# Windowed attention and a gated feed-forward block on one Trainium2 core: batch 2's q and k transposed by DMA, a new order of loads, batch 1 by token halves

## Chip, core and metric

The kernel runs on one core of one Trainium2 chip. The metric is the device time of one execution in microseconds (us). A profiled execution also has a span, from the first to the last recorded instruction; it is some 1.7 us shorter than the time. All executions compared below are in the fast state: none was over 1.5% above the fastest of its kernel, and the mean granted TensorE clock of a run was 0.96 to 1.0 of full speed.

## The reference

```python
# B, H, S, D = 4, 8, 768, 64;  n_sink = 4, window = 128
scores = (1 / sqrt(D)) * q @ k.T                 # per batch and head
keep   = is_sink(key) | (0 <= query - key < window)
a      = softmax(where(keep, scores, -1e9))
x      = (a @ v)           -> [3072, 512]        # tokens x (heads * D)
out    = (((x @ w1) * (x @ w2)) @ w3) @ w_out    # 512 -> 1024 -> 1024 -> 512
```

Inputs and output are fp32. A query sees four "sink" keys at the start and the 128 newest keys, so of the six key blocks of 128 only two and a strip are needed for each query block. Nothing stands between `@ w3` and `@ w_out`, so the kernel multiplies these two once into one matrix (the "fold") and uses that.

## The kernel before

All inputs are cast to bf16 while a DMA loads them. TensorE does, for each batch: transposes of q and k (so that the head dimension lies on partitions), score matmuls on 64 partitions, attention-value matmuls, transposes of x, then for each half of 384 tokens sixteen groups of four "gate" matmuls (w1 and w2) and the projection with the fold. VectorE and ScalarE share exps, masks, normalisation and the copies out of PSUM.

The order of instructions on each engine is not written by hand. Every piece of work is recorded as an `Op` with an estimated duration, its dependencies and the buffers that it takes; a list scheduler keeps a planned timeline (the "plan" below) and emits the operation that can start first:

```python
class Op:
    def __init__(self, eng, us, fn, deps=(), prio=0.0, takes=(), frees=(), ...): ...
# GpSimd issues the casting loads in exactly this order: k/q/v <batch>-<block>,
# w3j, w3 and wo: parts of w3 and w_out; w0..w3: quarters of w1 and w2
LOADS = """ident k0-0-4 q0-0-4 v0-2 w3j-0-1 tri v0-0 pick v0-1 wo-1-2 w3j-2-4 wo-0-1 w3j-1-2 wo-2-4
    w3j-4-6 wo-4-6 w3j-6-8 wo-6-8 w3-3 w3-5 w3-7 w2 w3-6 w0 w3-4 w3 k0-1-0 q0-1-0 v0-4 v0-3 ..."""
QK_BY_DMA, X_BY_DMA = (3,), (2, 3)     # batches whose q, k / whose x are transposed by DMA

# ... transposes of q and k of one batch, where TensorE does them: 2 x 4 groups of 6
a = Op(PE, cols(P, 6), tps, [...] + war, when(r / 4 + c / 50 - 0.1, 0), takes=["mm"])
tp_of[c, r] = Op(EITHER, (act_us(6 * P), dve_us(6 * P, 2)), tpc, [a], ...)     # the copy out of PSUM
# ... and where SyncE's queue does them: 12 DMA transposes of 128 x 512
nc.sync.dma_start_transpose(out=T[:, :, s, kb * P:(kb + 1) * P], in_=src[b][:, kb, :])

# ... the values of the four sink keys, spread to the rows where they are needed
def sv(b=b, x=x):
    nc.tensor.matmul(x[0].slot["mm"][:].rearrange("p (h d) -> p h d", d=D),
                     sel[:].rearrange("p r m -> p (r m)"), vN[b][:, 0, :, 0:D], start=True, stop=True)

# ... kind 0: attention for one half of the tokens, then for the other; kind 1: by heads over all tokens
kind = 0 if b == 0 else 1

# ... filler: TensorE multiplies zeros in gaps that the plan has before 45 us
if e == PE and start < 45.0 and start - free[PE] > 0.12:
    ...
        nc.tensor.matmul(view, zeros[:], zeros[:], start=True, stop=True)

# ... the last output tile leaves in two pieces of 256 columns
for n0, n1 in ([(0, 256), (256, 512)] if last else [(0, 512)]):
    ...
```

`EITHER` lets the scheduler choose VectorE or ScalarE. PSUM is shared: two double buffers `sc` for scores and the fold, one `av` for values, three `mm` for everything else.

The softmax here doesn't subtract the row's maximum and nothing guards it: scores larger than these inputs give would overflow.

## Time and profile before

| | before |
|---|---|
| time, median of the runs beside the changed kernel's | 203.46 us (203.09 to 203.55, 4 runs) |
| span of the profiled run | 201.6 us |
| mean granted TensorE clock | 0.997 |
| first gate matmul | 31.0 us |
| last matmul ends | 198.25 us |

The page's first rows give the busy time of each engine, and its chain rows say which engine ended last, followed back from the end. The prediction below shows those rows, the chain in order of time, the groups by shape, and the tail. In the group rows the second figure after the bar is the mean duration of one instruction, from start to end (219 ns for a 128-column transpose); what it costs TensorE in a stream is the smaller distance to the next start, 55.5 ns.

### The profile page before, as it was taken

What the parts mean: (1) busy time and instruction counts of PE and PEld (TensorE: products, weight loads), DVE (VectorE), ACT (ScalarE), POOL (GpSimd) and SP (SyncE); (2) the same over time, 40 slices, a digit from 0 to 9 for tenths busy, and PEclk for the clock granted to TensorE, in tenths of its full rate; (3) what the DMA queues carried; (4) which work ended last, traced back from release to release, by engine and by line L of the source; (5) the groups of instructions that cost most, each with busy time, mean ns of one, the idle gap of its engine ahead of it and who ended that gap; (6) DMA issues with size and microseconds to landing.
All of it is one profiled execution on the core that took longest, in us unless ns stands there. A gap on an engine that the chain in (4) does not pass through costs nothing.

```text
span 201.6 us, 4577 instructions
## 1 busy us (share of the span) xinstructions
PE 196.2 (97%) x1852; PEld 120.2 (60%) x1852; DVE 110.0 (55%) x252; ACT 108.3 (54%) x175; POOL 72.9 (36%) x96
## 2 busy tenths in 40 slices
PE   7999999999999999999999999999999999999993
PEld 6666555566676676666665654665565456556442
DVE  2586212377778989858876572884484214324200
ACT  3786634388578688984455354555532343343232
POOL 7976565488999899843000000000000000000000
PEclk9999999999999999999999999999999999999998
DMA  6999999999999999999999454101123630020124
GB/s 167 166 180 201 203 202 194 177 176 156 152 195 170 157 147 131 122 170 152 155 156 123 34 101 141 44 0 52 55 71 61 132 150 8 0 105 4 52 104 156
DMA packets 91349, 24.81 MB, mean 123 GB/s; under 512 B 80192, under 2 KB 87744, under 8 KB 91328
## 3 DMA queue, kind: packets, MB, share of 16 engines
q0 software_dynamic: 73584, 14.29, 96.1%
q1 hardware_dynamic: 17200, 9.84, 21.7%
q10 hardware_dynamic: 544, 0.39, 0.6%
q8 instruction: 14, 0.23, 0.5%
q14 instruction: 7, 0.06, 0.1%
HBM read 29.36 MB, written 6.29 MB: 177 GB/s over the span
## 4 chain that ended last, share of the span: by engine, by line
PE 91%; DMA 4%; POOL 1%; DVE 1%; ACT 0%; issue 0%; ACTq 0%; DVEq 0%
PE mm L679 42%; PE mm L709 20%; PE av L599 7%; PE sc L528 6%; PE mm L359 4%; DMA big<-in_moe_w_dram 3%; PE mm L432 3%; PE sc L329 2%; PE mm L635 1%; PE mm L352 1%; DMA out_dram<-o_sb 1%; PE mm L793 1%; PE mm L329 1%; PE mm L409 1%; PE mm L321 1%; POOL early L157 1%
## 5 line engine op out<-in xcount | busy, mean ns | idle before, releaser
L679 PE MATMUL mm<-xT,w_sb 128*128 128x384 bf16 x512 | 92.3, 326 | 0.0
L679 PEld LDWEIGHTS <-w_sb 128*128 128x128 bf16 x512 | 47.7, 98 | 33.3 <-issue 2.5
L694 DVE TENSOR_TENSOR ab<-a_sb,mm 128x384 bf16<-128x384 f32 x64 | 35.2, 552 | 43.8 <-PE mm L679 42.2
L541 ACT ACTIVATE ex<-sc 128x768 bf16<-128x768 f32 (+2 forms) x52 | 44.2, 895 | 7.7 <-PE sc L528 7.3
L709 PE MATMUL mm<-w3o,ab 128*128 128x512 bf16 (+1 forms) x200 | 46.4, 370 | 0.1
L140 ACT COPY a_sb<-mm 128x384 f32<-128x384 f32 x54 | 25.8, 481 | 37.6 <-PE mm L679 25.1
L547 DVE TENSOR_TENSOR am<-ex,maskt 128x768 bf16<-128x768 bf16 (+2 forms) x52 | 30.0, 595 | 1.3 <-ACT ex L541 1.2
L709 PEld LDWEIGHTS <-ab 128*128 128x128 bf16 x200 | 18.8, 98 | 18.2 <-issue 0.8
L140 ACT COPY o_sb<-mm 128x512 f32<-128x512 f32 (+1 forms) x23 | 13.1, 568 | 25.6 <-PE mm L709 23.4
L157 POOL DMA_DIRECT2D vN<-in_v_dram x24 | 21.4, 894 | 7.1 <-DMA big<-in_k_dram 2.7
L599 PE MATMUL av<-vN,am 128*128 128x65 bf16 x352 | 18.9, 193 | 0.0
L599 PEld LDWEIGHTS <-am 128*128 128x128 bf16 x352 | 16.9, 97 | 3.1 <-issue 0.5
L614 DVE TENSOR_TENSOR xs<-av,rec 128x384 bf16<-128x384 f32 x32 | 17.7, 553 | 0.6
L528 PE MATMUL sc<-qkT 64*128 64x256 bf16 (+1 forms) x248 | 14.8, 243 | 0.0
L140 ACT COPY qkT<-mm 128x384 bf16<-128x384 bf16 (+1 forms) x20 | 12.0, 642 | 4.4 <-PE mm L432 2.6
L599 PE MATMUL av<-vsb,es 128*128 128x130 bf16 x64 | 12.8, 219 | 0.0
L528 PEld LDWEIGHTS <-qkT 64*128 64x128 bf16 x248 | 8.1, 95 | 5.9 <-issue 4.5
L157 POOL DMA_DIRECT2D big<-in_k_dram x12 | 10.8, 904 | 1.2 <-PE mm L465 0.5
L157 POOL DMA_DIRECT2D big<-in_q_dram x12 | 10.8, 902 | 0.4 <-issue 0.2
L359 PE MATMUL mm<-big,w3t 128*128 128x512 bf16 x40 | 9.8, 379 | 0.0
L609 DVE RECIPROCAL rec<-av 128x6 f32<-128x6 f32 x32 | 6.2, 193 | 5.8 <-PE av L599 5.7
L140 DVE COPY a_sb<-mm 128x384 f32<-128x384 f32 x10 | 5.6, 555 | 6.7 <-PE mm L679 6.7
(65 smaller groups left out, 149.3 us busy)
## 6 DMA issues: line engine op xcount, KB each, us to landing
out_dram<-o_sb SPq DMA_DIRECT2D x23, 256.0 KB, 2.0
vN<-in_v_dram POOLq DMA_DIRECT2D x24, 128.0 KB, 7.0
w_sb<-in_moe_w_dram POOLq DMA_DIRECT2D x8, 256.0 KB, 10.1
big<-in_k_dram POOLq DMA_DIRECT2D x12, 128.0 KB, 7.1
big<-in_q_dram POOLq DMA_DIRECT2D x12, 128.0 KB, 7.2
big<-in_moe_w_dram POOLq DMA_DIRECT2D x5, 256.0 KB, 9.1
big<-in_moe_w_out_dram POOLq DMA_DIRECT2D x3, 256.0 KB, 7.9
near<-in_q_dram POOLq DMA_DIRECT2D x6, 128.0 KB, 6.7
```

The source lines that it names most:

```text
L140: (nc.scalar.copy if turn_of[0] == ACT else nc.vector.tensor_copy)(out, in_)
L157: op = Op(eng, us, lambda: (nc.gpsimd if eng == POOL else nc.sync).dma_start(out=out, in_=in_), deps)
L359: nc.tensor.matmul(x[2].slot["mm"][:], x[1].slot["w3t"][:, j, :], wo_sb[:, j, :], start=(j == 0), stop=(j == KFF - 1))
L528: nc.tensor.matmul(sc[:, e, c * P:(c + n) * P], T[hp, r, 0, kb * P:(kb + 1) * P], T[hp, r, 1, qb * P:(qb + n) * P], start=True, stop=True)
L541: nc.scalar.activation(y[1].slot["ex"][:, :, 0:w], y[0].slot[key][:, :, 0:w], ACTF.Exp, scale=scale)
L547: nc.vector.tensor_mul(y[2].slot["am"][:, :, 0:w], y[1].slot["ex"][:, :, 0:w], maskt[:, :, m0:m0 + w].to_broadcast([P, 2, w]))
L599: nc.tensor.matmul(o, lhs, rhs, start=(i == 0), stop=(i == len(todo) - 1), skip_group_check=True)
L609: nc.vector.reciprocal(x[1].slot["rec"][:], av_of(x[0].slot["av"])[:, :, :, D:VW])
L614: nc.vector.tensor_mul(xs_first[c].slot["xs"][:, :, r * P:(r + 1) * P].rearrange("p k (e d) -> p k e d", d=D), av_of(x[0].slot["av"])[:, : ...
L679: nc.tensor.matmul(pg[:, 0:TOK], w_sb[:, kk, dt * P:(dt + 1) * P], holder[0].slot["xT"][:, kk, :], start=(kk == 0), stop=(kk == NP - 1))
L694: nc.vector.tensor_mul(abh[0].slot["ab"][:, dt, :], y[1].slot["a"][:], y[2].slot["mm"][:, 0:TOK])
L709: nc.tensor.matmul(x[0].slot["mm"][:, 0:n1 - n0], abh[0].slot["ab"][:, kk, mi * P:(mi + 1) * P], w3o[:, kk, n0:n1], start=(kk == 0), stop= ...
```

## The change

The intent is to take 48 transposes of q and k and four sink matmuls from TensorE, the limit, and to give some of the freed time back to 24 transposes of x that DMA had done before. The loads are reordered so that the earliest work gets its data first, and loads of batch 3 are meant to stay behind those of batch 2 while batch 2's DMA transposes run. Batch 1 works by token halves, so its first half can go on before the second is loaded. The rest are small things: the tail in three pieces, value rows of even width, other weights in the scheduler's priorities (`LEAD`, `SPREAD`, `FOLD_J`, `FOLD_I`).

```diff
+    VP = D + 2
-    sel = home("sel", [P, H // 2, 32])
+    vst = home("vst", [P, B, D], FP32)
-    KA, LEAD, SPREAD = 3, -50, 0.8
-    QK_BY_DMA, X_BY_DMA = (3,), (2, 3)
+    KA, LEAD, SPREAD = 3, -120, 0.6
+    FOLD_J, FOLD_I = 990, 980
+    C_MAJOR = 2
+    QK_BY_DMA = (2, 3)
+    X_BY_DMA = ((3, 0), (3, 1))
 ... [eight small DMAs put the sink rows of v into vst]
+    LOADS = """w3j-1-2 tri k0-0-4 q0-0-4 wo-0-1 wo-2-4 ident v0-2 w3j-2-4 w3j-6-8 w3j-0-1 wo-1-2 pick
+        v0-1 wo-4-6 w3j-4-6 v0-0 w3-7 wo-6-8 w3-6 w3-5 w3-4 q0-1-0 k0-1-0 w0 w3-3 v0-5 w2 v0-3 w1
+        k1-1 k1-0 w3 k1-3 q1-1 v0-4 k1-2 q1-0 q2-0 q1-2 ... v3-0 v3-5"""
 ...
-        return t[:, 0:QC * 2 * VW].rearrange("p (k e d) -> p k e d", e=2, d=VW)
+        return t[:, 0:QC * 2 * VP].rearrange("p (k e d) -> p k e d", e=2, d=VP)
 ...
-        kind = 0 if b == 0 else 1
+        kind = 0 if b < C_MAJOR else 1
 ...
+            if b + 1 in QK_BY_DMA:                      # the hold
+                seen = []
+                for o in in_big:
+                    if o.batch == b:
+                        seen.append(next(t for t in tp_of.values() if o in t.deps))
+                    elif o.batch == b + 1:
+                        o.deps += seen[:-3]
 ...
-        def sv(b=b, x=x):
-            nc.tensor.matmul(x[0].slot["mm"][:] ..., sel[:] ..., vN[b][:, 0, :, 0:D], start=True, stop=True)
+        def sv(b=b, V=V):                               # VectorE, straight from vst
+            nc.vector.tensor_mul(V ..., vst[:, b:b + 1, :] ..., pick ...)
-        groups = [(2, 3), (3, 6)] if b < 1 else [(2, 6)]
+        groups = [(2, 3), (3, 6)] if kind == 0 else [(2, 6)]
 ...
-                for n0, n1 in ([(0, 256), (256, 512)] if last else [(0, 512)]):
+                for n0, n1 in ([(0, 256), (256, 384), (384, 512)] if last else [(0, 512)]):
 ... [the last piece is copied by ScalarE and issued on ScalarE's queue]
 ... [the scheduler keeps lists of ready operations instead of scanning all]
```

More of the change, by code (lines that the diff above doesn't have):

```diff
@@ L86 @@
         kN[b] = big[:, o + NQ:o + 2 * NQ].rearrange("p (k n) -> p k n", n=DM)
-    vN = homes("vN", B, [P, NB, H, VW + 1])
+    vN = homes("vN", B, [P, NB, H, VP])
     vsb = homes("vsb", 2, [P, NP, 2, VW])
@@ L212, with sink_v @@
     Op(DVE, 0.1, lambda: nc.vector.memset(zeros[:], 0.0))
+    op_v0 = Op(DVE, 0.3, lambda: nc.vector.memset(vst[:], 0.0), prio=-1)
+    op_vst = []
+    for h in range(H):
+        def sink_v(h=h):
+            p0 = 32 * (h // 2) + 4 * (h % 2)
+            nc.sync.dma_start(out=vst[p0:p0 + 4, :, :], in_=v[:, h, 0:4, :].rearrange("b s d -> s b d"))
+        op_vst.append(Op(SP, 0.45, sink_v, [op_v0], prio=-1))
+        op_vst[-1].turn = 0.05
     op_i1 = Op(DVE, 0.17, lambda: nc.vector.memset(ident[:], 1.0))
@@ L225 @@
                                          first_home[i][:, 0:TOK].rearrange("p (h m) -> p h m", h=2), st[i])
-    LOADS = """ident k0-0-4 q0-0-4 v0-2 w3j-0-1 tri v0-0 pick v0-1 wo-1-2 w3j-2-4 wo-0-1 w3j-1-2 wo-2-4
-        w3j-4-6 wo-4-6 w3j-6-8 wo-6-8 w3-3 w3-5 w3-7 w2 w3-6 w0 w3-4 w3 k0-1-0 q0-1-0 v0-4 v0-3
-        v1-3 w1 v0-5 q1-0 k1-3 k1-1 q1-1 k1-2 k1-0 v1-0 k1-4 q1-2 q1-4 k1-5 v1-2 q1-3 q1-5 v1-5
-        k2-2 k2-1 q2-1 v1-1 v1-4 k2-0 q2-0 k2-3 k2-4 q2-4 q2-2 k2-5 q2-5 v2-0 q2-3 k3-0 v2-4 v2-1
-        v2-2 v2-5 q3-0 v2-3 k3-1 q3-1 k3-2 q3-2 k3-3 q3-5 k3-5 q3-4 k3-4 v3-0 q3-3 v3-1 v3-4 v3-3
-        v3-2 v3-5"""
+    LOADS = """w3j-1-2 tri k0-0-4 q0-0-4 wo-0-1 wo-2-4 ident v0-2 w3j-2-4 w3j-6-8 w3j-0-1 wo-1-2 pick
+        v0-1 wo-4-6 w3j-4-6 v0-0 w3-7 wo-6-8 w3-6 w3-5 w3-4 q0-1-0 k0-1-0 w0 w3-3 v0-5 w2 v0-3 w1
+        k1-1 k1-0 w3 k1-3 q1-1 v0-4 k1-2 q1-0 q2-0 q1-2 k1-4 v1-0 q1-4 v1-5 k2-0 v1-2 v1-4 k2-3
+        v1-1 q1-5 k2-2 q2-2 v1-3 q2-4 q2-1 q1-3 k2-1 k1-5 v2-5 v2-2 k2-5 v2-0 k2-4 v3-1 q2-5 q2-3
+        q3-0 k3-3 v2-4 k3-2 v2-1 v2-3 k3-0 k3-4 k3-5 q3-2 k3-1 v3-2 q3-5 q3-1 v3-4 q3-3 q3-4 v3-3
+        v3-0 v3-5"""
     def masks(part):
@@ L250, in pick_cols @@
     def pick_cols():
-        nc.vector.memset(sel[:], 0.0)
-        for e in range(2):
-            nc.vector.tensor_copy(sel[0:4, :, 4 * e:4 * e + 4],
-                                  ident[0:4, None, 0:4].to_broadcast([4, NP, 4]))
         for i in range(2):
@@ L283 @@
                 kN if key[0] == "k" else qN, k if key[0] == "k" else q, n[0], n[1])
+            late.batch = n[0]
             if n[0] > 1:
@@ L295 @@
     op_mask = Op(DVE, 0.6, lambda: masks(1), [op_mask], prio=3)
-    op_sel = Op(DVE, 1.3, pick_cols, [op_pick, op_ident], prio=3)
+    op_cols = Op(DVE, 0.35, pick_cols, [op_pick], prio=3)
     op_bd = [Op(DVE, 0.11, lambda b=b: nc.vector.memset(ksbd[b][:], 0.0), prio=3 + 20 * b) for b in range(B)]
@@ L305, in av_of @@
     def av_of(t):
-        return t[:, 0:QC * 2 * VW].rearrange("p (k e d) -> p k e d", e=2, d=VW)
+        return t[:, 0:QC * 2 * VP].rearrange("p (k e d) -> p k e d", e=2, d=VP)
     fold_done = []
     hold = [None]
+    ACC = {3: ["sc", "mm"], 4: ["sc", "av", "mm"], 5: ["sc", "sc", "av"], 6: ["sc", "sc", "av", "mm"]}[KA]
+    acc_keys, n = [], 0
+    for i, name in enumerate(ACC):
+        wide = 2 if name == "sc" else 1
+        acc_keys.append((n, wide, (name, i) if ACC.count(name) > 1 else name))
+        n += wide
     def acc_of(n):
-        return hold[0].slot["mm"][:] if n == KA - 1 else hold[0].slot["sc"][:, n, :]
+        n0, wide, key = [a for a in acc_keys if a[0] <= n][-1]
+        t = hold[0].slot[key]
+        return t[:, n - n0, :] if wide == 2 else t[:]
     last = None
@@ L330, in fm @@
                                  start=(j == 0), stop=(j == KFF - 1), skip_group_check=True)
-        a = Op(PE, cols(P, KA), t3, [got["w3j", j], op_ident], 50 + j, takes=["mm"])
+        a = Op(PE, cols(P, KA), t3, [got["w3j", j], op_ident], FOLD_J + j, takes=["mm"])
         x.append(a)
-        cpy = Op(EITHER, (act_us(KA * P), dve_us(KA * P, 2)), t3c, [a], 50 + j, takes=["w3t"], frees=[(a, "mm")])
+        cpy = Op(EITHER, (act_us(KA * P), dve_us(KA * P, 2)), t3c, [a], FOLD_J + j, takes=["w3t"], frees=[(a, "mm")])
         x.append(cpy)
         last = Op(PE, cols(DM, KA), fm, [cpy, got["wo", j]] + ([last] if last else []),
-                  50.5 + j, takes=["sc", "mm"] if j == 0 else [], frees=[(cpy, "w3t")])
+                  FOLD_J + 0.5 + j, takes=ACC if j == 0 else [], frees=[(cpy, "w3t")])
         if j == 0:
@@ L340 @@
     first_fm = hold[0]
-    for i0, n_i, key in ((0, 2, "sc"), (2, 1, "mm")):
+    for i0, n_i, key in acc_keys:
         def fe(i0=i0, n_i=n_i, key=key):
@@ L363, in fmc @@
             copy(w3o[:, i, :], x[2].slot["mm"][:])
-        pr = 100 + 4 * i
+        pr = FOLD_I + 4 * i
         a = Op(PE, cols(P, KFF), t3, [got["w3", i], op_ident], pr, takes=["mm"])
@@ L440 @@
                            [got[n, b, QC * c + j] for n in "kq" for j in range(QC)] + [op_ident] + war,
-                           when(r / 4 + c / 50 - 0.1, 0), takes=["mm"])
+                           when((r / 4 + c) / 2 - 0.1 if kind == 0 else r / 4 + c / 50 - 0.1, 0), takes=["mm"])
                     x.append(a)
@@ L462 @@
         x = []
-        def sv(b=b, x=x):
-            nc.tensor.matmul(x[0].slot["mm"][:].rearrange("p (h d) -> p h d", d=D), sel[:].rearrange("p r m -> p (r m)"),
-                             vN[b][:, 0, :, 0:D], start=True, stop=True)
-        def svc(V=V, x=x):
+        def sv(b=b, V=V):
             nc.vector.tensor_mul(V[:].rearrange("p r e d -> p (r e) d")[:, :, 0:D],
-                                 x[0].slot["mm"][:].rearrange("p (h d) -> p h d", d=D),
+                                 vst[:, b:b + 1, :].to_broadcast([P, H, D]),
                                  pick[:, :, None].to_broadcast([P, H, D]))
         warv = list(all_av[b - 2]) if b >= 2 else []
-        a = Op(PE, cols(512), sv, [got["v", b, 0], op_sel] + warv, when(0, base + 2), takes=["mm"])
-        x.append(a)
-        op_sv = Op(DVE, dve_us(512), svc, [a, op_pick], base + 2, frees=[(a, "mm")])
-        groups = [(2, 3), (3, 6)] if b < 1 else [(2, 6)]
+        op_sv = Op(DVE, dve_us(512), sv, op_vst + [op_cols] + warv, when(0, base + 2))
+        groups = [(2, 3), (3, 6)] if kind == 0 else [(2, 6)]
         op_es = {}
@@ L493 @@
             a = Op(PE, cols(w) + 0.22, ss, [op_sk] + sum([tdep(c, r) for c in cs for r in range(NP)], []) + warv,
-                   when(0, base + 2), takes=["mm"])
+                   when(0.5 if q0 == 3 else 0, base + 2), takes=["mm"])
             x.append(a)
@@ L504 @@
                     two = [(r, 2 * c), (r, 2 * c + 1)]
-                    tasks += [two] if c else [[t] for t in two]
+                    tasks += [two] if c or b else [[t] for t in two]
         else:
@@ L512 @@
             x = []
-            us = 0.2
+            us = 0.13
             deps = []
@@ L529, in scv @@
                                              T[hp, r, 1, qb * P:(qb + n) * P], start=True, stop=True)
-            s_ = Op(PE, us, scv, deps, when(n_v / 6, base + 4 + 0.01 * n_v), takes=["sc"] * len(visit))
+            s_ = Op(PE, us, scv, deps, when(n_v / len(tasks), base + 4 + 0.01 * n_v), takes=["sc"] * len(visit))
             x.append(s_)
@@ L590, in avf @@
                     if qb >= 2:
-                        todo.append((av[:, qi, :, :], es[b % 2][:, (qb - 2) * P:(qb - 1) * P], V[:, r, :, :]))
+                        todo.append((av[:, qi, :, 0:VW], es[b % 2][:, (qb - 2) * P:(qb - 1) * P], V[:, r, :, :]))
                     for kb in (qb - 1, qb):
@@ L595, in avf @@
                             for e in range(2):
-                                todo.append((av[:, qi, e, :], m_.slot["am"][:, e, off:off + P],
+                                todo.append((av[:, qi, e, 0:VW], m_.slot["am"][:, e, off:off + P],
                                              vN[b][:, kb, 2 * r + e, 0:VW]))
@@ L624 @@
             holder = [None]
-            if b not in X_BY_DMA:
+            if (b, c) not in X_BY_DMA:
                 evs = []
@@ L640, in xtc @@
                                               transposed(x[1].slot["mm"], 6 * P).rearrange("p (r m) -> p r m", r=2))
-                    a = Op(PE, cols(P, 6), xtp, [norm[c, 2 * n_h], norm[c, 2 * n_h + 1]], when(n_h / 2 + 0.5, base + 2.5), takes=["mm"],
+                    a = Op(PE, cols(P, 6), xtp, [norm[c, 2 * n_h], norm[c, 2 * n_h + 1]], when(c / 2 + (n_h + 1) / 4 if kind == 0 else n_h / 2 + 0.5, base + 2.5), takes=["mm"],
                            frees=[(xs_first[c], "xs")] if n_h else [])
@@ L702 @@
                 x = []
-                last = b == B - 1 and m == NB - 1
-                for n0, n1 in ([(0, 256), (256, 512)] if last else [(0, 512)]):
+                last, oh = b == B - 1 and m == NB - 1, []
+                for n0, n1 in ([(0, 256), (256, 384), (384, 512)] if last else [(0, 512)]):
                     x = []
@@ L715, with pcopy, pout @@
                             frees=[(abh, "ab")] if mi == QC - 1 and n1 == 512 else [])
-                    def pcopy(n0=n0, n1=n1, x=x):
-                        copy(x[1].slot["o"][:, n0:n1], x[0].slot["mm"][:, 0:n1 - n0])
-                    pc = Op(EITHER, (act_us(n1 - n0), dve_us(n1 - n0)), pcopy, [p2], 0, takes=["o"], frees=[(p_, "mm")])
-                    x.append(pc)
-                    def pout(b=b, m=m, n0=n0, n1=n1, x=x):
+                    def pcopy(n0=n0, n1=n1, x=x, oh=oh):
+                        copy(oh[0].slot["o"][:, n0:n1], x[0].slot["mm"][:, 0:n1 - n0])
+                    end = last and n1 == DM
+                    pc = Op(ACT if end else EITHER, act_us(n1 - n0) if end else (act_us(n1 - n0), dve_us(n1 - n0)), pcopy, [p2] + oh, 0, takes=[] if oh else ["o"],
+                            frees=[(p_, "mm")])
+                    oh.append(pc)
+                    def pout(b=b, m=m, n0=n0, n1=n1, oh=oh, end=end):
                         t0 = b * S + m * P
-                        nc.sync.dma_start(out=out[t0:t0 + P, n0:n1], in_=x[1].slot["o"][:, n0:n1])
-                    Op(SP, 0.1, pout, [pc], 0, frees=[(pc, "o")]).turn = 0.8 * (n1 - n0) / 512
+                        (nc.scalar if end else nc.sync).dma_start(out=out[t0:t0 + P, n0:n1], in_=oh[0].slot["o"][:, n0:n1])
+                    Op(ACT if end else SP, 0.4, pout, [pc], 0, frees=[(oh[0], "o")] if n1 == DM else []).turn = 0.8 * (n1 - n0) / 512
     free = {PE: 1.0, ACT: 0.8, DVE: 0.9, POOL: 0.9, SP: 0.8}
     WARM = 5.8
-    pending = {e: [o for o in ops if e in o.us_on] for e in free}
+    for o in ops:
+        before = o.deps + ([o.after] if o.after is not None else [])
+        o.missing, o.users = len(before), getattr(o, "users", [])
+        for d in before:
+            d.users = getattr(d, "users", [])
+            d.users.append(o)
+    in_order = [o for o in ops if POOL in o.us_on]
+    ready = {e: [o for o in ops if e in o.us_on and not o.missing] for e in free}
     def unsure(at):
@@ L735, in wants @@
     def wants(o):
-        at = 0.0
-        if o.after is not None and o.after.done is None:
-            return None
-        for d in o.deps:
-            if d.done is None:
-                return None
-            at = max(at, d.done + HOP)
-        need = {}
-        for n in o.takes:
-            need[n] = need.get(n, 0) + 1
-        for n, k_ in need.items():
+        at = max([d.done + HOP for d in o.deps], default=0.0)
+        for n in set(o.takes):
+            k_ = o.takes.count(n)
             f = sorted(x for x in rings[n].free if x is not None)
@@ L753, in best @@
     def best(e):
-        if not pending[e]:
-            return None
-        if e == POOL:
-            o = pending[e][0]
-            w = wants(o)
-            return None if w is None else (max(w, free[e]), o)
         pick_ = None
-        for o in pending[e]:
-            w = wants(o)
+        for o in ready[e]:
+            w = wants(o) if e != POOL or o is in_order[0] else None
             if w is None:
@@ L824 @@
             for e_ in o.us_on:
-                pending[e_].remove(o)
+                ready[e_].remove(o)
+            if e == POOL:
+                in_order.pop(0)
+            for u in o.users:
+                u.missing -= 1
+                if not u.missing:
+                    for e_ in u.us_on:
+                        ready[e_].append(u)
             left -= 1
```

## The prediction

> **What bounds the kernel now.** I read the page first (busy shares, slices, chain), then the chain in order of time, then the TensorE groups with their shapes kept apart, then the timeline of the first 42 us with the GpSimd rows, and last the tail. From the page:
>
> ```profile
> PE 196.2 (97%) x1852; PEld 120.2 (60%) x1852; DVE 110.0 (55%) x252; ACT 108.3 (54%) x175; POOL 72.9 (36%) x96
> ...
> DMA  6999999999999999999999454101123630020124
> ...
> PE 91%; DMA 4%; POOL 1%; DVE 1%; ACT 0%; issue 0%; ACTq 0%; DVEq 0%
> ```
>
> TensorE is busy 97% and is 91% of the chain that ended last; VectorE and ScalarE are little over half busy. The DMA row adds that some DMA engine is busy throughout the first 110 us of 201.6: loads are a second resource there. So I price the change in TensorE time and then ask where TensorE has nothing useful to do. The record of one matmul overlaps the next, so a price must be a start-to-start interval, not a mean duration. The chain in order of time gives those:
>
> ```profile
> 38.29 2.60 PE mm L679 x16
> ...
> 52.30 0.54 PE av L599 x15
> ...
> 59.38 1.06 PE mm L432 x18
> ...
> 64.90 0.37 PE av L599 x11
> ...
> 140.74 1.73 PE mm L709 x8
> ```
>
> That is 0.1625 us for a gate matmul (384 columns), 0.216 for a projection or fold matmul (512), 0.36 and 0.54 for the two attention-value groups, and 1.06/18 = 0.059 for a 128x128 transpose (0.0555 where six follow one another, 0.34/6). Counts come from the groups by shape:
>
> ```profile
> L793 PE MATMUL mm<-zeros 128*128 128x128 bf16 x71 | 7.6, 271 | 1.2 <-DVE zeros L212 1.1 <-DVE vsb L469 0.2
> ...
> L635 PE MATMUL mm<-ident,xs 128*128 128x128 bf16 x48 | 4.0, 219 | 0.0
> L432 PE MATMUL mm<-ident,big 128*128 128x128 bf16 x48 | 3.8, 219 | 0.1
> ...
> L465 PE MATMUL mm<-vN,sel 128*128 128x512 bf16 x4 | 1.5, 378 | 0.0
> ```
>
> Multiplying every group by its interval (gates 83.2, projections 41.4, fold 13.8 + 3.6 of transposes, attention scores 12, values 14.6, the rest 14) gives about 182.5 us of useful TensorE work; the 84 matmuls on zeros are filler and not counted. The last matmul ends near 198.1, so 15.6 us are lost. Where: when the first gate starts at 31.0, 18.7 us of useful work have been done, so 12.3 of the 15.6 are lost before 31 us (start, cold array, waiting for weights) and only 3.3 after. The tail behind the last matmul is 201.6 - 198.1 = 3.5 us.
>
> **What the Trainium skill says.** "TensorE: Matmul & The Clock Gate", section Back-to-back issue gap, gives an isolated warm gap of N/2.4 + 2.5 ns: 56, 162.5 and 216 ns for 128, 384 and 512 columns. The trace has 55.5, 162.5 and 216: it agrees. It also quotes 131 ns sustained for 512 columns, which this trace doesn't show. "DMA: Bandwidth & Descriptors", section Issuing engines are not separate DMA queues, says DMAs of all issuing engines run on the same 16 DMA engines; the trace agrees in that a q/k transpose took 8.5 us to land among loads and an x transpose 2.5 us when the loads were over. "VectorE: DVE Perf Modes", section Why PSUM operands drop a tier, caps fp32 from PSUM at the plain rate: the normalisation (384 fp32 from PSUM) takes 553 ns, as slow as other fp32 reads of that width, so I give rows of even width nothing.
>
> **The change, part by part.** The built programs can be compared in order and count, without times.
> - Batch 2's q, k by DMA: 48 transposes leave TensorE, 48 x 0.0555 = -2.7 us, and eight copies of 0.55 to 0.80 us leave VectorE and ScalarE (about 5.4 us, off the path but in the busiest stretch for them, 75 to 88 us).
> - Batch 2's x goes back from DMA to TensorE: 24 transposes more, +1.3 us, and four copies of 0.56 to 0.80.
> - The rows for the sink values come by eight tiny DMAs instead of a matmul: 4 x 0.216 = -0.9 us.
> - Batch 1 by token halves: 112 score matmuls of 256 columns and 128 of 128 instead of 104 and 144, the same columns; two smaller sink-score groups for one. +0.2 us.
> - The last tile's output in pieces of 256, 128, 128 with the last one issued by ScalarE's queue: the last copy falls from 0.37 us to about 0.27, and the last piece no longer needs a free buffer. In the tail below the second half's copy started only on the release of a buffer, but the last matmul had ended just before that, so this is 0.2 to 0.4 us, not 2.
>
> ```profile
> 197.88 0.37 ACT L140 COPY o_sb<-mm 128x256 f32<-128x256 f32 x1 [0.72 <-PE mm L709]
> 198.44 0.37 ACT L140 COPY o_sb<-mm 128x256 f32<-128x256 f32 x1 [0.18 <-DMA out_dram<-o_sb]
> ```
>
> Useful TensorE work: 182.5 - 2.7 - 0.9 + 1.3 + 0.2 = about 180.3.
> - The order of the loads: this one costs. GpSimd waits for an earlier load before each issue, which dates the landings:
>
> ```profile
> 17.55 0.76 POOL L157 DMA_DIRECT2D w_sb<-in_moe_w_dram  x1 [0.59 <-DMA big<-in_moe_w_out_dram]
> ...
> 22.12 0.74 POOL L157 DMA_DIRECT2D w_sb<-in_moe_w_dram  x1 [0.60 <-DMA big<-in_moe_w_out_dram]
> ...
> 25.81 0.74 POOL L157 DMA_DIRECT2D w_sb<-in_moe_w_dram  x1 [0.51 <-DMA big<-in_moe_w_dram]
> ```
>
> 256 KB land per 1.27 us. Before, the last piece for the fold's first part was 2560 KB down the list and landed at 22.1; now it is at 2816 KB. The first fold matmul needed 1188 KB and came at 15.4; now it needs 1472 KB. The weights of the first gates end at 3840 KB before and at 4864 KB now. GpSimd's first issue comes about 0.8 us earlier, which gives back some 0.5. Laying the new TensorE order against these landings, the first fold matmul comes near 17.0, the first part's last near 25, and then the second fold part, its transposes and batch 0's other half run densely up to the first gate near 34.5, with 20.9 us of useful work done: 13.6 us lost there, against 12.3. +1.3 us. The added filler (120 matmuls on zeros instead of 84) sits in those waits and costs little.
> - After that the order is dense. Batch 2's scores need all twelve DMA transposes. Its last q block is the 33rd load after the last weights (issued near 36), at about 1.05 us a load: issued near 71, landed near 79, transposed by 88. TensorE reaches these scores near 93. Loads for batch 1's first half are due near 51 against a use near 54. The margins are 3 to 5 us, so I expect the stalls after the first gate to fall from 3.3 to about 2.3, because the copies that delayed TensorE at 77 to 82 us (0.6 for an x copy, 0.7 for an output copy) thin out.
> - The hold on batch 3's loads: no GpSimd instruction of the built program waits on a transpose's semaphore. The hold exists in the scheduler's plan only, so batch 3's loads will share the DMA engines with batch 2's transposes. I give it 0.
>
> **Sum.** 180.3 + 13.6 + 2.3 = 196.2 for the last matmul's end, + 3.2 of tail = 199.4 span, against 201.6: -2.2. On the time 203.39 that is 201.2; I shade it to 200.9, because the tail pieces and the relieved copies may give a little more.
>
> **Rivals.**
> - *The start eats it all.* If the first gate comes at 36 or later (value rows of batch 0 arrive after most of the fold's weights, so its first attention group moves from 12.8 us to near 20), the loss at the start is 15 to 16 us and the time is 202.5 to 203.5. For: loads run without a break up to 38 us. Against: the second fold part can be done meanwhile.
> - *Batch 2 comes late.* The transposes wait behind loads, as batch 3's did before (8.5 us each), and TensorE stands before batch 2's scores for 3 to 8 us: 204 to 208. For: the hold is nominal, and the queue of SyncE is in order, so a late block blocks outputs too. Against: 5 us of margin.
> - *Everything meshes.* The middle stalls vanish (-3.3) and the start costs nothing: 182.5 to 180.3, plus the stalls, 197.5 to 198.5. For: VectorE and ScalarE lose 5 us in their busiest stretch. Against: the landings above.
>
> **Range and chances.** The removed matmuls are sure to a few tenths; the start (+-1.5) and the middle (+-1.5) are not. Range 198.0 to 203.6. Over 2% faster means under about 199.4, which needs both start and middle to go well: 0.28. Slower by 2% needs the second rival: 0.04. Within 2%: 0.68.
>
> **What would show it.** Transposes of q, k on TensorE 48, of x 72, no matmul for the sink values; the first gate near 34.5 with the deficit of useful work 13.6; no TensorE gap of a microsecond before batch 2's scores near 93; batch 2's transposes landing before 90 while batch 3's loads are still issued; the last copy near 0.27 us. A first gate before 32, or a gap before batch 2's scores, would make the prediction wrong.

## The result

| | before | after |
|---|---|---|
| time, median | 203.46 us (203.09 to 203.55, 4 runs) | 201.79 us (201.26 to 202.19, 4 runs) |
| ratio after / before | | 0.992 (0.9891 to 0.9948) |
| span of the profiled run | 201.6 | 200.5 |
| first gate matmul | 31.0 | 34.1 |
| last matmul ends | 198.25 | 197.05 |

A ratio here, and in all that follows, is the mean time of one kernel's fast runs over the mean of the other's in the same rounds, with its 95% interval; it is therefore not quite the ratio of the medians. The change saves 0.8%, which counts as the same at a threshold of 2%, and 201.8 lies inside the predicted range.

From the page of the changed kernel, the same three rows as the prediction shows of the kernel before:

```profile
PE 193.9 (97%) x1864; PEld 119.0 (59%) x1864; DVE 111.7 (56%) x260; ACT 104.1 (52%) x171; POOL 73.1 (36%) x96
...
DMA  6999999999999999999999982002101563000133
...
PE 91%; DMA 4%; POOL 3%; DVE 0%; issue 0%; ACT 0%; POOLq 0%
```

The bound has not moved: TensorE is 97% busy and 91% of the chain. Its busy time fell by 2.3 us, although it now contains 120 filler matmuls where it had 84. The DMA row stays full a little longer, to about 115 us instead of 110. The groups by shape confirm the counts:

```profile
L654 PE MATMUL mm<-ident,xs 128*128 128x128 bf16 x72 | 6.0, 219 | 0.0
L450 PE MATMUL mm<-ident,near 128*128 128x128 bf16 x48 | 3.8, 219 | 0.0
```

The q, k transposes that are left (`near`) are batch 1's, x has 72 instead of 48, and no sink matmul exists any more. The start is in the TensorE timeline. Columns: start, duration, engine, line, operation, output and inputs, shapes, count; before and after:

```profile
30.98 0.81 PE L679 MATMUL mm<-xT,w_sb 128*128 128x384 bf16 x4
```

```profile
16.86 0.60 PE L347 MATMUL sc<-big,w3t 128*128 128x512 bf16 x2
...
33.70 0.50 PE L547 MATMUL sc<-qkT 64*128 64x128 bf16 x8
34.14 0.82 PE L698 MATMUL mm<-xT,w_sb 128*128 128x384 bf16 x4
```

The first gate comes 3.2 us later. That is not a loss of 3.2 us, since fold work and attention of batch 0 were drawn forward. I counted every TensorE group that starts before the first gate and priced it with the start-to-start intervals of the prediction. The whole span then divides as follows:

| TensorE, us | before | after | change | predicted change |
|---|---|---|---|---|
| useful work, priced by intervals | 183.0 | 181.3 | -1.7 | -2.2 |
| lost before the first gate | 11.6 | 12.8 | +1.2 | +1.3 |
| lost after it, up to the last matmul's end | 3.65 | 2.95 | -0.7 | -1.0 |
| tail behind the last matmul | 3.35 | 3.45 | +0.1 | -0.3 |
| span | 201.6 | 200.5 | -1.1 | -2.2 |

(The recount of before differs by 0.5 to 0.8 from the rounder one in the prediction; the changes are what matters.) Three of the four terms came in a little worse than expected. The experiments and the trace tell why.

### The profile page after: what moved, and what is told of

The parts are those of the page before. It is cut to its first block, busy times and chain, and to the rows that moved or that the text cites. A ratio compares the mean times of both kernels' runs of the same rounds, so it can differ in the third digit from the quotient of the medians.

```text
span 200.5 us, 4622 instructions
## 1 busy us (share of the span) xinstructions
PE 193.9 (97%) x1864; PEld 119.0 (59%) x1864; DVE 111.7 (56%) x260; ACT 104.1 (52%) x171; POOL 73.1 (36%) x96
## 4 chain that ended last, share of the span: by engine, by line
PE 91%; DMA 4%; POOL 3%; DVE 0%; issue 0%; ACT 0%; POOLq 0%
PE mm L698 42%; PE mm L728 21%; PE av L618 7%; PE sc L547 5%; PE mm L377 4%; DMA big<-in_moe_w_dram 4%; PE mm L654 2%; PE sc L347 2%; PE mm L450 2%; PE mm L370 1%; POOL big L158 1%; PE mm L347 1%; PE mm L427 1%; POOL early L158 1%; PE mm L339 1%; PE mm L504 1%
## 5 line engine op out<-in xcount | busy, mean ns | idle before, releaser
L698 PE MATMUL mm<-xT,w_sb 128*128 128x384 bf16 x512 | 91.2, 326 | 0.0
L560 ACT ACTIVATE ex<-sc 128x768 bf16<-128x768 f32 (+2 forms) x56 | 44.8, 845 | 9.6 <-PE sc L547 8.6
L141 ACT COPY a_sb<-mm 128x384 f32<-128x384 f32 x55 | 26.4, 479 | 40.9 <-PE mm L698 25.4
L728 PE MATMUL mm<-w3o,ab 128*128 128x512 bf16 (+2 forms) x208 | 46.1, 363 | 0.0
L566 DVE TENSOR_TENSOR am<-ex,maskt 128x768 bf16<-128x768 bf16 (+2 forms) x56 | 30.7, 561 | 2.0 <-ACT ex L560 2.0
L141 ACT COPY o_sb<-mm 128x512 f32<-128x512 f32 (+2 forms) x20 | 10.8, 544 | 22.1 <-PE mm L728 21.9
L807 PE MATMUL mm<-zeros 128*128 128x128 bf16 x99 | 9.1, 248 | 1.3 <-DVE zeros L216 1.3
L807 PEld LDWEIGHTS <-zeros 128*128 128x128 bf16 x120 | 8.6, 111 | 2.5 <-DVE zeros L216 1.3
L141 DVE COPY qkT<-mm 128x384 bf16<-128x384 bf16 (+1 forms) x13 | 6.9, 553 | 5.5 <-PE mm L427 3.1
```

The costliest lines, as they stand in the source:

```text
L141: (nc.scalar.copy if turn_of[0] == ACT else nc.vector.tensor_copy)(out, in_)
L560: nc.scalar.activation(y[1].slot["ex"][:, :, 0:w], y[0].slot[key][:, :, 0:w], ACTF.Exp, scale=scale)
L566: nc.vector.tensor_mul(y[2].slot["am"][:, :, 0:w], y[1].slot["ex"][:, :, 0:w], maskt[:, :, m0:m0 + w].to_broadcast([P, 2, w]))
L698: nc.tensor.matmul(pg[:, 0:TOK], w_sb[:, kk, dt * P:(dt + 1) * P], holder[0].slot["xT"][:, kk, :], start=(kk == 0), stop=(kk == NP - 1))
L728: nc.tensor.matmul(x[0].slot["mm"][:, 0:n1 - n0], abh[0].slot["ab"][:, kk, mi * P:(mi + 1) * P], w3o[:, kk, n0:n1], start=(kk == 0), stop= ...
```

## The experiments

Each kernel below is the changed kernel with one edit, unless said otherwise. All gave a correct result. The runs were made in three calls, each on another chip, so kernels are compared through their ratios to the kernel before, run in the same rounds; a ratio difference of 0.01 is 2.0 us. An edit here also changes what the scheduler plans, so unless it is said that the order stayed the same, a result is that of the edit with its new order. No run puts back the sink matmuls or the old priorities by themselves.

| run | median us | ratio to before | 95% interval |
|---|---|---|---|
| after_again: no edit | 201.79 | 0.9923 | 0.9893 to 0.9953 |
| work_back | 204.83 | 1.0088 | 1.0070 to 1.0107 |
| qk2_on_pe | 205.23 | 1.0102 | 1.0082 to 1.0121 |
| no_hold | 203.19 | 1.0006 | 0.9990 to 1.0022 |
| b1_heads | 216.53 | 1.0659 | 1.0612 to 1.0707 |
| loads_before | 202.32 | 0.9964 | 0.9946 to 0.9983 |
| hybrid | 202.94 | 0.9987 | 0.9970 to 1.0003 |
| no_filler | 202.83 | 0.9972 | 0.9949 to 0.9994 |
| x2_by_dma | 206.02 | 1.0128 | 1.0090 to 1.0166 |
| tail_before | 201.92 | 0.9939 | 0.9918 to 0.9961 |
| odd_rows | 202.17 | 0.9944 | 0.9924 to 0.9965 |
| x21_tuned | 201.17 | 0.9902 | 0.9882 to 0.9921 |

**after_again.** The changed kernel unedited, as the base of the comparisons.

> The changed kernel once more, unedited, as the control of this series and to see how much it varies. All theories: 201.2 to 202.0, ratio to before 0.992.

It repeats the first result (0.9923 against 0.992), so the saving of 0.8% is real; its interval runs from 0.5% to 1.1%.

### Is the saving TensorE work, or the relief of the copies?

Theory: what counts is the 48 transposes taken off TensorE, 2.7 us. Rival: the eight copies out of PSUM that go with them had delayed TensorE, and their absence is the gain. Two kernels tell these apart. The first puts batch 2's transposes and copies back:

```diff
-    QK_BY_DMA = (2, 3)
+    QK_BY_DMA = (3,)
```

> The changed kernel with batch 2's q and k transposed on TensorE again (48 transposes and 8 copies back). Theory A: 48 x 0.0555 = 2.7 us more, 204.0 to 205.0. Rival B (TensorE has slack in that stage, the gain came from copies and transfers): under 202.6. Rival C (load list): 201.8.

The second gives TensorE 48 matmuls on zeros of the same shape, at the same place in the order and with the same waits for the loads, but no copies; the DMA transposes stay:

```diff
+            if b == 2:
+                for c in range(NC):
+                    for r in range(NP):
+                        def again(x=x):
+                            for i in range(6):
+                                nc.tensor.matmul(x[0].slot["mm"][:, 0:P], zeros[:], zeros[:], start=True, stop=True)
+                        a = Op(PE, cols(P, 6), again, [got[n, b, QC * c + j] ...] + war, when(r / 4 + c / 50 - 0.1, 0), takes=["mm"])
+                        a.frees.append((a, "mm"))
```

> The changed kernel with 48 matmuls of 128 columns on zeros put where batch 2's transposes stood before; nothing copies their result, and DMA still transposes. Theory A: the same 2.7 us more as with real transposes, 204.0 to 205.0; the copies themselves cost nothing. Rival B (it is the copies on VectorE and ScalarE whose removal gained): 201.8 to 202.6 here while qk2_on_pe is dearer by over a microsecond.

```profile
L486 PE MATMUL mm<-zeros 128*128 128x128 bf16 x48 | 3.2, 219 | 0.0
```

The dummy matmuls are all there, with the 219 ns of a transpose, and cost 1.0088 - 0.9923 = 3.4 us; with the copies as well it is 3.6 us. The copies by themselves are worth at most some tenths, within the scatter. So the theory holds and the rival falls: VectorE and ScalarE had room. The 3.4 us exceed 48 x 0.0555 = 2.7. In the trace the dummies take 2.74 us from start to start, and the last matmul ends 3.1 us later than in after (200.15 against 197.03) with the first gate at the same time. Part of the rest is the new order: it enters score or sink groups 26 times after the first gate instead of 24, at some 0.1 us each way (a price worked out further below). What is left is a few tenths and not settled.

### What does the hold on batch 3's loads do?

The prediction gave it nothing, since in the built program no GpSimd instruction waits for a transpose.

```diff
-                        o.deps += seen[:-3]
+                        pass
```

> The changed kernel without the hold of batch 3's loads. GpSimd's instructions and their waits are the same, word for word, as in the changed kernel; only the plan, and so the order on the other engines, differs. Theory A: no effect of the transfers, 201.4 to 202.3. Rival D (the hold protects batch 2's transposes): those land later than before, TensorE stands before batch 2's scores, 203 or more.

The time rose by 0.0083, 1.7 us, so the hold matters, although GpSimd's instructions and the number of waits of each came out identical in the two traces. It doesn't act on the transfers: the VectorE copy that is the first user of batch 2's transposed k stands at nearly the same time, after first and no_hold second:

```profile
90.49 0.49 DVE L483 COPY ksbd<-qkT 64x16 bf16<-64x16 bf16 x2
```

```profile
90.31 0.49 DVE L483 COPY ksbd<-qkT 64x16 bf16<-64x16 bf16 x2
```

What changed is the plan. A list scheduler that believes in later landings puts other work ahead. In no_hold the order brings TensorE to gates of batch 2 while the copy of their x still runs on ScalarE, which the chain shows:

```profile
124.36 0.35 PE mm L654 x6
124.73 0.81 ACT xT L141
125.58 0.82 PE mm L698 x4
```

The transposes of x, then 0.81 us in which the chain runs through the ScalarE copy, then the gates. This wait of 1.05 us (timeline), one of 0.40 at 126.2 and one of 0.57 at 61 (0.19 there in after) add up to 1.8 us more than after has, enough for the loss. So the prediction's "0" was wrong by 1.4 to 1.7 us, though its reason, that no wait is emitted, was right. Since the sum of the prediction was made on the built order, with the hold in it, the error didn't enter that sum.

### Batch 1 by halves or by heads?

```diff
-    C_MAJOR = 2
+    C_MAJOR = 1
```

> The changed kernel with batch 1's attention by heads again, everything else kept. The sum of TensorE's work alone (two score groups and one sink-score group fewer) gives 0.5 us less: 201.0. Theory E (the halves are there so that gates of batch 1 can start early enough to lie between the score groups): the plan now puts score and value groups of batches 1 and 2 back to back with few gates between, TensorE waits for the exponentials on ScalarE, and the time is 203 or more with gaps between score groups.

This was far worse, 216.5 us. The two rows below are of the TensorE timeline (the bracket is the idle time before and what ended it) and of the windows view (busy time and count for PE, PEld, DVE, ACT, POOL, then the granted clock, the DMA share and GB/s):

```profile
95.75 0.62 PE L504 MATMUL mm<-qkT,ksbd 128*32 128x512 bf16 x4 [4.64 <-DMA qkT<-big]
```

```profile
75.00:105.00 30.00, 21.07 (x275) 14.11 (x273) 18.03 (x40) 19.93 (x26) 18.22 (x21) 0.83 1.91 165
```

TensorE ran out of work at 91 us and waited 4.64 us for batch 2's DMA transposes, the prediction's second rival in pure form. Of those 30 us it was busy for 21. Besides the 4.64 us, 2.3 us of the idle time are two waits of value matmuls for VectorE's normalisation (1.37 before 85.6, 0.88 before 98.9), and 1.7 are five short waits of score groups for exps. The granted clock fell to 0.83; after's row for the same window has TensorE busy for 30.00 and a clock of 1.00. So working by halves is not a gain of its own; counted in groups it costs some tenths (see below). It is what makes work available until batch 2's transposes have landed. The parts of the change hang together.

### What does the order of the loads cost and bring?

Theory: the new list costs about 1.3 us at the start. The first kernel has the whole old list:

```diff
-    LOADS = """w3j-1-2 tri k0-0-4 q0-0-4 wo-0-1 wo-2-4 ident v0-2 ...   [the new list]
+    LOADS = """ident k0-0-4 q0-0-4 v0-2 w3j-0-1 tri v0-0 pick v0-1 ...   [the old list]
```

> The changed kernel with only the list of loads put back as it was in the kernel before. Theory A (the time is TensorE's useful work plus what is lost before the first gate, and the new list costs 1.0 us at the start): the first gate comes back from 34.1 us to about 31 with the lost part at 12.3 instead of 13.25 us, and the time is 200.5 to 201.2, unless batch 2's blocks, which the old list brings later, make a new wait. Rival C (the new list is what gained): 203 or more, with TensorE gaps in the middle.

The first gate came at 31.2 and 12.1 us were lost before it instead of 12.8: the cost of the new list at the start is there, 0.7 us of it. Yet the time is not better but rather worse (0.9964 against 0.9923; the intervals overlap only just). The profiled span was 200.2, shorter than after's, while the 22 timed runs reach from 201.3 to 204.1. My reading is that the old list leaves thinner margins later on and pays for it in some runs, but this one profile doesn't show which wait makes the slow ones slow, so that stays open.

The next kernel tried to have both: the old list up to the last weights, then the new order.

```diff
-    LOADS = """w3j-1-2 tri k0-0-4 q0-0-4 ... w3j-4-6 v0-0 w3-7 ... w3 k1-3 q1-1 v0-4 k1-2 q1-0 q2-0 ...
+    LOADS = """ident k0-0-4 q0-0-4 v0-2 w3j-0-1 ... w3 k0-1-0 q0-1-0 v0-4 v0-3 v1-3 w1 v0-5 k1-1 k1-0 k1-3 q1-1 ...
```

> The changed kernel with the old list up to the last weights and the new list's order for the rest. Theory A: the start gains what loads_before gained (lost part before the first gate 12.1 us against 12.8), without that run's spread of 201.3 to 204.1 us, so 200.8 with a spread under 1 us. If the spread stays, it comes from the head of the list and not from the late blocks of batches 1 and 2.

It missed: 0.9987, no better than the kernel before. Value matmuls waited for a late v block (0.60 us at 64), transposes of batch 1 for a late k block (0.28 us at 74.7), and a copy of x delayed gates at 125.0 by 0.40. These are 1.3 us together, and score or sink groups are entered 27 times after the first gate instead of 24; the better start (first gate at 30.8) doesn't make up for it. A good start and a good middle don't add up here.

### The filler at the start

The changed kernel has 120 matmuls on zeros instead of 84, and I had said that they cost little. This kernel leaves out those that the plan puts after 5.8 us, 84 of them, with all else in the same order:

```diff
-            if e == PE and start < 45.0 and start - free[PE] > 0.12:
+            if e == PE and start < WARM and start - free[PE] > 0.12:
```

> The changed kernel without its 84 matmuls on zeros after the first 36; every other instruction stands in the same order on every engine. Theory G (a gap on TensorE lowers the granted clock, as the gaps of x2_by_dma and b1_heads did, 0.71 and 0.83 in those stretches): the matmuls between 8 and 25 us run slower, the first gate comes 1 us or more later than 34.1, and the time is 202.5 or more. Rival (the filler is only there to look busy; the start is bound by the loads): 201.8.

The windows view of 8 to 17 us, after first and no_filler second:

```profile
8.00:17.00 9.00, 7.87 (x133) 6.13 (x130) 6.10 (x16) 6.75 (x13) 7.63 (x14) 1.00 1.56 184
```

```profile
8.00:17.00 9.00, 6.32 (x66) 3.45 (x66) 6.00 (x17) 6.75 (x13) 8.10 (x15) 0.80 1.55 181
```

Without the filler the granted clock is 0.80 in this window, and 0.80 again in the next, 17 to 25 us, although TensorE is busy for 7.96 of those 8 us: up to 20.2 fold matmuls started 0.43 us apart instead of 0.22. The first gate came 0.7 us later and the time rose by about 1.0 us (the two intervals overlap only just; the clock and the first gate point the same way). So the filler pays.

### x of batch 2: TensorE or DMA?

The change gave TensorE 24 transposes, 1.3 us, that DMA had done. This kernel gives them back to DMA:

```diff
-    X_BY_DMA = ((3, 0), (3, 1))
+    X_BY_DMA = ((2, 0), (2, 1), (3, 0), (3, 1))
```

> The changed kernel with batch 2's x transposed by DMA, as it was before the change. Theory A (TensorE's work is the time): 24 x 0.0555 = 1.3 us less, 200.2. Rival F (x goes through the same in-order queue as the transposes of batch 3's q and k, and the gates of batch 2 wait for it): TensorE stands before the first gates of batch 2, 202 or more.

It lost 4.2 us. From the SyncE rows of the timeline, then its TensorE rows, then the windows view:

```profile
118.68 1.21 SPq L468 DMA_TRANSPOSE qkT<-big  x1
120.00 1.20 SPq L674 DMA_TRANSPOSE xT<-xs  x1
```

```profile
126.73 0.40 PE L547 MATMUL sc<-qkT 64*128 64x128 bf16 x6 [0.91 <-ACT ex L560]
...
132.71 1.47 PE L698 MATMUL mm<-xT,w_sb 128*128 128x384 bf16 x4
```

```profile
125.00:135.00 10.00, 7.47 (x87) 4.36 (x88) 6.66 (x13) 8.19 (x11) 0.00 (x0) 0.71 0.41 107
```

VectorE had normalised the first half of x by 119.2 us. Its first transpose went out at 120.0, right behind the last one of batch 3's q and k, and SyncE was done with the third at 126.4, because each occupies SyncE for 1.2 us and output DMAs stand between them; in after, TensorE does its last six transposes of that half at 119.2 in 0.3 us. The first gates of batch 2 come at 132.7 instead of 121.8. No wait stands right before them: the plan had put batch 3's scores and values first. Those scores, with two buffers, wait for the exps of ScalarE (0.91 us here), and although no such gap exceeds 1 us, the granted clock falls to 0.71 in this window (0.50 from 129.3 to 136), against 1.00 in the same window of after. The Trainium skill has this on "TensorE: Matmul & The Clock Gate", section A second HAM failure mode: psum-queue depth-cycling, for a kernel whose TensorE idles shortly and often between groups as it goes round its PSUM buffers. This trace agrees. So the 24 transposes are well paid for here, where q and k of two batches share that queue with x and the outputs.

### The tail and the even rows

```diff
-                for n0, n1 in ([(0, 256), (256, 384), (384, 512)] if last else [(0, 512)]):
+                for n0, n1 in ([(0, 256), (256, 512)] if last else [(0, 512)]):
-                    end = last and n1 == DM
+                    end = False
```

> The changed kernel with the last tile sent in two halves by SyncE, as before the change. The prediction gave the three pieces 0.2 to 0.4 us: then 202.1 here. Rival (the 3.4 us from the last matmul to the end are the transfer's landing and the end of the program, which the pieces don't shorten): 201.8.

The last copy of after, in the ScalarE rows of the timeline:

```profile
197.07 0.27 ACT L141 COPY o_sb<-mm 128x128 f32<-128x128 f32 x1 [0.18 <-PE mm L728]
```

The copy fell from 0.37 to 0.27 us as predicted, but from the last matmul's end to the end of the span it is 3.45 us, against 3.4 with two pieces (last matmul at 196.8, span 200.2). Of this, 3.1 us (3.0 with two pieces) come after the copy: the last issue and its landing, which a smaller piece doesn't shorten. The times don't differ either.

```diff
-        return t[:, 0:QC * 2 * VP].rearrange("p (k e d) -> p k e d", e=2, d=VP)
+        return t[:, 0:QC * 2 * VW].rearrange("p (k e d) -> p k e d", e=2, d=VW)
```

> The changed kernel with attention's value rows 65 wide again in PSUM; the same instructions in the same order, only addresses differ. As predicted, even width is worth nothing: 201.8, the normalisation still 553 ns. Rival: it was worth something, then the normalisation or its reciprocal is slower here and the time is over 202.3.

The normalisation takes 554 ns with rows of 65 and 553 with rows of 66, and the reciprocal 193 and 192. The even width brings nothing to the operations that read it; the times (0.9944 and 0.9923) are not resolved.

### A version that follows from these

If SyncE's queue is what stops x of batch 2 from going by DMA, half of it may still fit. This kernel gives the second half's 12 transposes to DMA and reorders the later loads for that. The order was found by trying swaps against the kernel's own plan, which serves to choose a candidate and proves nothing:

```diff
-    X_BY_DMA = ((3, 0), (3, 1))
+    X_BY_DMA = ((2, 1), (3, 0), (3, 1))
-    LOADS = """... q0-1-0 k0-1-0 w0 w3-3 v0-5 w2 v0-3 w1 k1-1 k1-0 w3 k1-3 q1-1 v0-4 k1-2 ...
+    LOADS = """... q0-1-0 k0-1-0 w0 w2 w3-3 k1-1 q1-1 w1 v0-3 v0-4 w3 k1-0 k1-3 v0-5 q1-0 ...
```

> A candidate for a better kernel: the second half of batch 2's x by DMA (12 transposes of 0.0555 us less on TensorE), and the order of the late loads shifted until the kernel's own plan had no new gap on TensorE. Theory A: 0.7 us less, 201.1. Theory G's warning: if one of the new waits is real on the chip, 202 or more.

It has the lowest time of all, 201.17 us and a span of 199.4, and is faster than the kernel before beyond doubt. The 12 transposes fewer are worth 0.7 us, and the first gate comes at 33.7. Against the changed kernel (0.9902 to 0.9923, measured in different calls) the intervals overlap, so that it beats this one is likely but not shown.

## Why the prediction was right or wrong

**The bound and the class: right.** TensorE was and is the limit, and the sum of small terms left the change within 2%. No rival came about in the kernel itself: the first gate came well before 36 us, and batch 2 wasn't late. The second rival is real in neighbouring kernels, though: batch 2 comes late in b1_heads, and in x2_by_dma batch 2's x comes late through SyncE's queue.

**The removed transposes: right in kind.** Putting their work back cost 3.4 us where the step said 2.7.

**Useful work, -2.2 predicted, -1.7 measured.** The term that was too small is batch 1 by halves, put at +0.2 because the columns are the same. It makes eight score groups out of six, and one more group for the sinks. From first score to next full-height matmul, batch 1's groups take 3.84 us instead of 3.39, which is the 0.5 of this row; two more groups are also entered, at 0.1 each, which is lost in the middle. The term was thus some 0.65 instead of 0.2. A group has a price besides its columns, as the point on the middle shows.

**The start, +1.3 predicted, +1.2 measured.** The first fold matmul (17.0 predicted, 16.86 measured), the end of the fold's first part (25, about 24.6) and the first gate (34.5, 34.1) came near the predicted dates, and the loss is as predicted. The reason given is only partly right. One sum is off: before, the list up to the first fold's block of w_out holds 1312 KB and not 1188 (it landed at 15.35 us, just before that fold matmul), so the 17.0 is in part luck. And these are the chain's lines of after where it leaves the DMA:

```profile
6.46 7.61 DMA big<-in_moe_w_dram
14.07 0.04 issue
14.11 0.34 PE mm L339 x3
```

From there to the first gate the chain stays on TensorE, filler included. The last of the first gates' weights landed at 32.8, 1.4 us before the gate. So after 14.1 us the planned order, which has the landings in it as estimates, set the dates, and not a landing itself.

**The middle, -1.0 predicted, -0.7 measured: the copies did delay TensorE, but by less than half of what was read from the chain.** The step said that copies delayed TensorE at 77 to 82 us, 0.6 for x and 0.7 for the output, since the chain listed them. These are the chain's lines of the kernel before, and then what its TensorE did there (timeline):

```profile
77.11 0.57 DVE xT L140
...
81.12 0.70 DVE o_sb L140
```

```profile
76.84 0.81 PE L679 MATMUL mm<-xT,w_sb 128*128 128x384 bf16 x4
77.72 1.02 PE L709 MATMUL mm<-w3o,ab 128*128 128x512 bf16 x4
...
80.92 1.44 PE L432 MATMUL mm<-ident,big 128*128 128x128 bf16 x18
82.29 0.39 PE L528 MATMUL sc<-qkT 64*128 64x128 bf16 x6
```

Four gate matmuls from 76.84 last 4 x 0.1625 = 0.65, to 77.49, and the projection starts at 77.72: 0.23 us are lost, not 0.57. Eighteen transposes from 80.92 last 1.0, and the scores start at 82.29: 0.37 lost, not 0.70, and 0.1 of it is the step to a score group that is priced below. The chain goes through the copies because they released what came next, but TensorE was working in the meantime on something else. A piece of the chain on another engine is not a gap of the bound engine. In after these two losses are gone. What makes most of the 3 us "lost" after the first gate, in both kernels, is this (TensorE's timeline, before and after):

```profile
65.11 0.81 PE L679 MATMUL mm<-xT,w_sb 128*128 128x384 bf16 x4
65.85 0.62 PE L528 MATMUL sc<-qkT 64*128 64x128 bf16 x12
66.40 1.48 PE L679 MATMUL mm<-xT,w_sb 128*128 128x384 bf16 x8
```

```profile
63.95 0.81 PE L698 MATMUL mm<-xT,w_sb 128*128 128x384 bf16 x4
64.70 0.45 PE L547 MATMUL sc<-qkT 64*128 64x256 bf16 x6
65.08 1.47 PE L698 MATMUL mm<-xT,w_sb 128*128 128x384 bf16 x8
```

Four gate matmuls cost 4 x 0.1625 = 0.65, but the scores start 0.74 and 0.75 after them. From the last gate to the first score it is 0.258 us instead of 0.1625: 0.1 us lost on the way in. Score matmuls use 64 rows of the array, gates all 128, and the way back costs as much: the last 128-column score is 0.148 from the next gate, where such pairs follow each other 0.052 apart. After the first gate TensorE goes in and out 23 times before and 24 times after, at 0.096 each way. The ways in are 2.2 and 2.3 us of the lost time; the ways out, another 2 us or so, are in the price of the score groups. No thinning of copies can remove either.

**Batch 2's transposes: the dates were early, the margin was enough.** From GpSimd's and SyncE's rows of the timeline of after:

```profile
77.26 0.88 POOL L158 DMA_DIRECT2D big<-in_q_dram  x1 [0.33 <-DMA vN<-in_v_dram]
```

```profile
63.11 23.68 SPq L468 DMA_TRANSPOSE qkT<-big  x9
```

The last q block was issued at 77.3 instead of 71, as a load takes nearer 1.2 us than 1.05. The run of nine transposes from 63.1 ends at 86.8, and the copy at 90.5 shown above waits for the last, so they had landed by about 90 and not 88. TensorE reached batch 2's scores at 95.4, predicted 93, and did not stand. The margin was some 5 us because both were late together, which is luck.

**The tail, -0.3 predicted, +0.1 measured.** The copy shrank by the 0.1 us that was reckoned; the rest of the gain, from the free buffer and the other queue, did not come.

**The hold: 0 predicted, 1.4 to 1.7 us in fact**, through the plan.

Together: the span was predicted at 199.4 and measured at 200.5. The 1.1 us are 0.5 of useful work, 0.3 of the middle and 0.4 of the tail, less 0.1 of the start. The prediction as recorded expected 200.9 against 203.39, -2.5; the medians differ by 1.7. The further shading of the time to 200.9 for the tail and the copies was unfounded, as tail_before and work_back show.

## What to carry to other kernels

Price a change to a TensorE-bound kernel in start-to-start intervals and add a price for each change between narrow and full-height groups (0.1 us each way here); then look in the timeline whether a piece of the chain on another engine is a gap at all. Work taken off the bound engine pays in full only while other work fills the wait for the engine that does it instead: the same 48 transposes save 3.4 us with batch 1 by halves, and without these halves the kernel stands still for 4.6 us at once and loses clock as well. Where a planner fixes the order, an edit that leaves the loads and their waits alone can still move the time by nearly a per cent (0.8% in no_hold), so compare the built orders and test each part by itself.

## What the Trainium skill lacked or had wrong

- "TensorEngine Tiling (Array Packing)", section Key Properties, says that changing the tiling mode drains TensorE and gives no price. Here, the step from a full-height matmul to a group on 64 rows took 0.258 us instead of 0.1625, and the step back 0.148 instead of 0.052; both fit such a drain at 0.096 us, paid 23 to 24 times each way after the first gate. That it is the drain is an inference from the page; the runs show the time alone.
- "VectorE: DVE Perf Modes", section The three transpose paths, lists 390 ns for a 128x128 bf16 transpose on TensorE. In a stream here it costs 55 to 59 ns of TensorE's time (219 ns from start to end of one), and a DMA transpose of 128x512, which does the work of four, occupied SyncE for 1.2 us, 0.3 each, where the table has 1309 ns for one. Both figures of the table are thus far above what a stream pays here; the ratio is about 5 instead of 3.4 in TensorE's favour, without the copies out of PSUM.
- No page that I read prices short idling: with gaps of under 1 us each, the granted clock was 0.71 over 10 us in x2_by_dma, and 84 matmuls on zeros raised it from 0.80 to 1.00 at the start, worth about 1.0 us.
